# RWKV5 attention and SwiGLU on one core: an opening in another order, a hint for the closing branch, and six closing stores

## The chip, the cores and the metric

The kernel runs on one NeuronCore of a Trainium2 chip. The metric is the device time of one execution in microseconds (us). The five engines named below are PE (matrix multiply), PEld (its weight loads), DVE (vector), ACT (scalar), POOL (GpSimd) and SP, which here only issues DMA transfers. Each engine takes its instructions strictly in the order of its own queue and waits on semaphores for the others.

## The reference

Two blocks stand one behind the other. The first is an RWKV5 attention over 4 batches, 8 heads, 768 steps and head size 48:

```python
for t in range(S):
    kt, vt, rt = k[:, :, t], v[:, :, t], r[:, :, t]
    cur = einsum('bhd,bhe->bhde', u[None] * kt, vt)
    y[:, :, t] = einsum('bhd,bhde->bhe', rt, state + cur)
    state = w[None, :, :, None] * state + einsum('bhd,bhe->bhde', kt, vt)
```

The result is laid out as x, 3072 tokens by 384 columns, and goes through a SwiGLU feed-forward with 1536 hidden columns:

```python
g = x @ w_gate
out = (g / (1 + exp(-g)) * (x @ w_val)) @ w_out
```

The three weight matrices arrive as 64-bit floats; r, k, v, w and u are 32-bit.

## The kernel before

**Items.** The sequence is cut into six chunks of 128 steps. With four batches that makes 24 items; item i is chunk i // 4 of batch i % 4. In each item the recurrence becomes matrix products: keys and receptances are scaled by powers of the decay w and turned (transposed) by PE, their product gives a 128 by 128 score matrix for each head (`scores`, L454), a mask keeps its strict triangle, the diagonal gets the products of r, u and k (`diagonal`, L364 on ACT and L371 on POOL), and `outputs` (L507) multiplies the scores with v, and the turned receptances with the state. `update` (L522 on PE, L532 to L535 on DVE and POOL) carries the state to the next chunk.

**The scalings.** DVE works out two tables of powers in turned layout. For items 0 to 3 PE turns the raw k and r and DVE multiplies by the tables on the way out of PSUM (L387). The same tables are turned back once (`natural_tables`, L349) and kept by ACT (`keep_natural_tables`, L353); with them POOL scales keys and receptances in natural layout (`scale_k` L341, `scale_r` L344), and the later items are turned after scaling and copied by ACT (L389). The products of r, k and u for the diagonal are made on POOL (`own_begin` L254, `own_end` L257) and summed on DVE (`own_sum` L265).

**The weights.** They come in 18 chunks of 768 KB (`load_weights`, L179), first and second alternately from w_gate and w_val, then w_out. Each is rounded from 64 to 32 bits by ACT (`round_high` L199, `round_low` L205), DVE (`round_dve` L214 and L215) and POOL (`add_low` L223, or `round_pool` L242 for a whole chunk).

**The feed-forward.** Gate and value units (L545) start as soon as a first pair of weight chunks is rounded and two items have their outputs; `feed` runs them between the attention's steps. Sums over weights and activations are used to save products; the closing part ("tail") consists of `three_units` (L801 on PE) and `project_thirds` (L1027 on PE, evictions L1020 and L1022), whose last pieces store the rows to the output (L995).

**What sets the order.** The scheduling is manual: the function `fast` writes out the program, and the order of calls is the order in each engine's queue. What the tile pools leave open is only waiting. SP's queue issues nearly all loads, one behind the other, so a load that waits for a buffer holds up all loads behind it. The opening, from `load(0)` to the loop over s, is written out call by call. `warm(n)` puts n identity products on PE; each is recorded as two matmuls.

**The end.** At the twelfth step the kernel counts the values of w outside the range that its tables can take, and leaves the count in `outside`. After `fast`, each of the five engines loads this count into a register (L1375) and compares and branches (L1376): where the count is above zero, a general version of the whole kernel, whose code stands between, is run; here it is zero, and the branch jumps over that code. Behind it SP waits for the others and the closing barrier ends the program.

Of the kernel before, what the change touches and what calls it, by code (L numbers as in the profile page):

```python
# [15 lines left out]
P = 128  # L16
# [6 lines left out]
def fast(  # L23
# [24 lines left out]
    nc = tc.nc  # L48
# [7 lines left out]
    DM, DFF = moe_w_gate.shape  # L56
# [86 lines left out]
    def load_v(i):  # L143
        c, b = divmod(i, B)
        for e in range(2):
            for p, a, o in places(i, HP):
                rows = slice(P * c + p.start + o, P * c + p.stop + o)
                sp.dma_start(
                    out=v_ld[i % 4][p, a, 64 * e : 64 * e + D],
                    in_=v[b, :, rows, :].rearrange("(a e) t d -> e t a d", e=2)[e][:, a],  # L150
                )
# [22 lines left out]
    def load_weights():  # L174
        n = next_chunk("load")
        if n is not None:
            src = chunks[n][0].bitcast(INT32)
            bits[n] = three.tile([P, WN, 2], INT32, name="w_bits", tag="w_bits")
            sp.dma_start(  # L179
                out=bits[n][:].rearrange("p (c f) two -> p c (f two)", c=src.shape[1]), in_=src  # L180
            )
# [81 lines left out]
    def own_sum(i):  # L263
        dus[i] = three.tile([P, H], FP32, name="du", tag="du")
        dve.tensor_reduce(dus[i][:], rks.pop(i), axis=AX.X, op=ALU.add)  # L265
# [18 lines left out]
    load(0)  # L284
    load(1)
    load_weights()
    load_v(0)
    load_weights()
    load_v(1)

    act.activation(sg0[:], ident[:, 0:1], AF.Silu)
    def warm(n, bank=None):

        ps = next_psum(HP, P)[:, 0, :] if bank is None else bank[:, 0:P]
        for _ in range(n):
            pe.matmul(ps, ident[:], ident[:], start=True, stop=True)  # L296

    warm(12)
    u_ps = next_psum(CC, P).rearrange("p c t -> p (c t)")
    pe.matmul(u_ps, ones_row, u_row, start=True, stop=True)  # L300
    act.copy(ub.rearrange("p h d -> p (h d)"), u_ps)
    next_psum(CC, P)
    warm(4)

    pool.memset(mask[:], 1.0)
    pool.affine_select(
# [39 lines left out]
    def natural_tables():  # L346
        for bank, t in zip(banks, (pw[:, :, 1 : P + 1], pv)):
            for a in range(HP):
                pe.transpose(bank[:, P * a : P * a + P], t[:, a, :], ident[:])  # L349
# [29 lines left out]
    def turn(i):  # L379
        kr = khat[i % 4], rhat_of(i)  # L380
        tps = [next_psum(HP, P) for _ in kr]
        turned[i] = three.tile([P, HP, P], FP32, name="rT", tag="rT")
        for tp, t, dst, table in zip(tps, kr, (kT[i % 2], turned[i]), (pw[:, :, 1 : P + 1], pv)):
            for a in range(HP):
                pe.transpose(tp[:, a, :], pair(t, a), ident[:])  # L385
            if i < 4:
                dve.tensor_mul(dst[:], tp[:], table)  # L387
            else:
                act.copy(dst[:], tp[:])  # L389
# [569 lines left out]
    def project_thirds(g):  # L959

        ends = g + 2 == N // 2
        A, B_, C, D_, E, F = room["h"]
        (x00, x01), (x10, x11), (x20, x21) = (
            [third(hTs, k, j) for j in range(2)] for k in range(3)
        )
        h = {
            "r3": A, "r4": B_, "r1": C, "r0": D_, "r8": E, "r10": F, "r14": A, "r13": B_,
            "r12": C, "r2": D_, "r6": E, "r5": x00, "r7": x21, "r9": x20, "r11": x11,
        }
        rows = hv[:, NR + 6 : NR + 12].rearrange("p (q r) t -> p q (r t)", q=2)  # L970
        c = [rows[:, :, DM * (k % 2) + P * (k // 2) :][:, :, 0:P] for k in range(6)]
        made = {
            0: [(dve.tensor_sub, E, x01, x11)],
            1: [(dve.tensor_add, F, x01, x21)],
            2: [(dve.tensor_add, A, x10, x20)],
            3: [(dve.tensor_sub, B_, x00, F)],
            4: [(dve.tensor_add, C, B_, x20)],
            5: [(dve.tensor_sub, D_[q], D_[q], x20[:, q]) for q in range(2)],
            6: [(dve.tensor_add, E[:, q], D_[q], x21[:, q]) for q in range(2)],
        }  # L980
        used = {
            "r3": [("copy", 2)], "r4": [("copy", 1)], "r1": [("copy", 0)], "r0": [("sub", 2)],
            "r8": [("copy", 3), ("sub", 1)], "r10": [("copy", 5)], "r14": [("copy", 4)],
            "r12": [("add", 0)], "r13": [("add", 4)], "r2": [("add", 5)], "r6": [("add", 3)],
            "r9": [("sub", 4)], "r5": [("sub", 0), ("sub", 1)], "r11": [("add", 2), ("add", 3)],
            "r7": [("add", 5)],
        }
        lasts = ("r4", "r0", "r8", "r9", "r5", "r11", "r7")
        open_ = {}

        def store(q, j):
            cc, b = divmod(2 * (g + q) + j, B)
            n0 = S * b + P * cc
            issue = sp if ends and q == 0 else act
            issue.dma_start(out=out[n0 : n0 + P, :], in_=rows[:, q, DM * j : DM * j + DM])  # L995

        def make(n):
            for op, o, a, b in made.get(n, ()):
                op(o, a, b)
            if not ends:  # L1000
                prepare_threes(g + 2, n)

        def item(n):
            what, chain = THIRDS[n]
            if n:
                make(n)
            first = chain not in open_
            split = ends and chain == "l5"
            if first:
                open_[chain] = [take()] + ([ring_a.popleft()] if split else [])  # L1010
            banks_ = open_[chain]

            def evict(q):
                for how, k in used[what]:
                    x = banks_[0][:, 0 : 2 * P].rearrange("p (q t) -> p q t", q=2)
                    if split:
                        x = banks_[q][:, q * P : q * P + P]
                    o = c[k][:, q] if split else c[k]
                    if how == "copy":
                        act.copy(o, x)  # L1020
                    else:
                        (dve.tensor_add if how == "add" else dve.tensor_sub)(o, o, x)  # L1022

            for q in range(2):
                ps = banks_[q if split else 0][:, q * P : q * P + P]
                for f in range(4):
                    pe.matmul(  # L1027
                        ps, (h[what][q] if h[what] is D_ else h[what][:, q])[:, f, :], wide["o"][what][:, f, :],
                        start=first and f == 0 and (split or q == 0), stop=f == 3, skip_group_check=True,
                    )  # L1030
                if split:
                    evict(q)
                    if what == "r7":
                        store(q, 1)
            if not split:
                evict(None)
            if n == 0:
                for do in wide.pop("last"):
                    do()
                make(0)  # L1040
            if what in lasts:
                free.append(banks_[0])
            if what == "r11":
                store(0, 0)
                store(1, 0)
            if what == "r7" and not split:
                store(0, 1)
                store(1, 1)
        return [lambda n=n: item(n) for n in range(15)]
# [149 lines left out]


    turn(0)
    own_sum(0)
    own_begin(1)
    diagonal(0)
# [1 line left out]
    flush()  # L1206
    load(2)
    turn(1)
    natural_tables()
    round_high(0, 0, 0)  # L1210
    round_low(0)
    load(3)
# [14 lines left out]
    add_low(1, 0)  # L1227
    own_product(2)
    outputs(1)
    keep_natural_tables()  # L1230
    scale_k(0)
    scale_k(1)
    queue(0)
# [4 lines left out]
        del bits[n], lows[n]  # L1238
    done.update(act=2, pool=2)
    load_weights()  # L1240
    turn(2)
    feed(1)
    own_sum(2)
    diagonal(2)
    flush()
    own_product(3)
    turn(3)
    dve.tensor_copy(w128[:].unsqueeze(2), pw[:, :, 0:1])
    warm(3, free[0])
    scores(2)  # L1250
    update(0)
    update(1)
    feed(1)
    own_sum(3)
    diagonal(3)
    flush()
    scores(3)
    scale_k(2)
    outputs(2)
    load(4)  # L1260
    round_act()
    scale_k(3)
    outputs(3)
    round_act()
    round_pool()
    update(2)
    update(3)
    scale(4)
    load_v(4)
    feed(1)  # L1270
    round_pool()
    own_product(4)
    load(5)
    feed(1)
    own_sum(4)
    round_act()
# [80 lines left out]
    tail = threes[0] + projections[0][:-2]  # L1357
    tail += threes[1][0:1] + projections[0][-2:-1] + threes[1][1:2] + projections[0][-1:]
    tail += threes[1][2:] + projections[1]
    for piece in tail:  # L1360
        piece()


@with_exitstack
def kernel(
    ctx: ExitStack,
    tc: tile.TileContext,
    *args: bass.AP,
):
    nc = tc.nc  # L1370
    ctx.enter_context(tc.manual_schedule())
    flag = ctx.enter_context(tc.tile_pool(name="flag", bufs=1))
    outside = flag.tile([1, 1], INT32, name="outside")
    fast(tc, *args, outside[:])
    n = nc.values_load(outside[:], min_val=0, max_val=512)  # L1375
    with tc.If(n > 0):  # L1376
        general(tc, *args)


# [395 lines left out]
```

## Time and profile before

| | us |
|---|---|
| median of 3 runs (lowest, highest) | 595.56 (594.47, 597.43) |
| the profiled execution | 594.87 |
| its span on the core | 593.1 |
| PE busy | 580.1 |
| PEld busy | 521.0 |
| DVE busy | 421.7 |
| POOL busy | 355.1 |
| ACT busy | 225.8 |

The mean clock granted to PE was 0.997 of full speed. The span runs from the first to the last record of the core; the execution's own time is 1.8 us longer.

Lines of the profile are read as follows. A line of the timeline gives the start, the length, the engine, the line of the kernel, the operation, output and inputs by name, shapes and a count of merged instructions; the bracket at its end gives the idle time of that engine just before, and the instruction that ended it. An engine's name followed by q stands for its sequencer: the issue of a DMA, a register load, a branch or a semaphore wait. In the page's slices each digit is the busy share of one fortieth of the span, in tenths. The chain is followed back from the last instruction to what released each one.

### The profile page before, as it was taken

Reading aid. Unit: us, or ns where it says so; the run is one execution under the profiler, and the core shown is the slowest. Engines: PE = TensorE matmul, PEld = TensorE weight load, DVE = VectorE, ACT = ScalarE, POOL = GpSimd, SP = SyncE. Lnnn points to the kernel's source line nnn. Section 1 sums busy time; section 2 is a strip of 40 time slices with the busy share of each in tenths; the row PEclk is TensorE's granted clock in tenths of the full one; section 3 lists DMA queues with packets and bytes.
Section 4 is the critical chain, followed back from the end, with each engine's and each line's share of the span. In section 5 each row is a group of like instructions: output and inputs, shape, how many; then the busy total and the mean of one; then the engine's idle time right before and its main releaser. Section 6 shows DMA issues by size and latency. Waiting matters only on the chain.

```text
span 593.1 us, 13229 instructions
## 1 busy us (share of the span) xinstructions
PE 580.1 (98%) x5234; PEld 521.0 (88%) x5234; DVE 421.7 (71%) x703; ACT 225.8 (38%) x517; POOL 355.1 (60%) x378
## 2 busy tenths in 40 slices
PE   8989999999999999999999999999999999999995
PEld 7778888899888899988899988889988899988895
DVE  7867887489488877577887477779257877377672
ACT  3468886321343422244332344423134320233310
POOL 6789889989999503977601996513678960010600
PEclk9999999999999999999999999999999999999998
DMA  8979887732342323233234233200100000100001
GB/s 198 254 177 252 236 287 87 86 65 48 75 74 35 54 48 68 49 62 57 39 60 82 60 54 54 48 12 3 54 1 1 1 1 1 55 0 1 1 2 59
DMA packets 148009, 41.53 MB, mean 70 GB/s; under 512 B 138465, under 2 KB 141794, under 8 KB 147938
## 3 DMA queue, kind: packets, MB, share of 16 engines
q1 hardware_dynamic: 144770, 36.27, 30.4%
q10 hardware_dynamic: 3168, 4.33, 2.0%
q8 instruction: 43, 0.70, 0.5%
q14 instruction: 28, 0.23, 0.1%
HBM read 28.31 MB, written 4.72 MB: 56 GB/s over the span
## 4 chain that ended last, share of the span: by engine, by line
PE 88%; POOL 4%; DVE 2%; SPq 2%; DMA 1%; issue 1%; ACT 1%; POOLq 0%; DVEq 0%
PE bank L801 28%; PE bank L620 18%; PE ring L801 13%; PE bank L1027 9%; PE bank L545 8%; PE ring L507 5%; PE ring L454 3%; SPq L411 2%; POOL wgv L242 1%; POOL s L731 1%; PE ring L522 1%; PE ring L296 1%; PE ring L385 1%; DMA r_ld<-in_r_dram 1%; POOL hats L344 0%
## 5 line engine op out<-in xcount | busy, mean ns | idle before, releaser
L825 DVE TENSOR_TENSOR hv<-hv,bank 128x512 f32<-128x512 f32 x132 | 87.1, 681 | 25.7 <-PE bank L801 14.8
L545 PE MATMUL bank<-xT,wgv 128*128 128x256 f32 x288 | 66.3, 384 | 0.0
L801 PE MATMUL bank<-xf,wgv 128*128 128x256 f32 x256 | 65.9, 382 | 0.0
L364 ACT ACTIVATE At<-ident,du 128x128 f32<-128x128 f32 x176 | 59.8, 396 | 14.8 <-DVE du L265 6.4
L825 ACT COPY hv<-bank 128x512 f32<-128x512 f32 x72 | 40.1, 585 | 58.6 <-PE bank L801 52.3
L545 PEld LDWEIGHTS bank<-xT,wgv 128*128 128x128 f32 x288 | 53.4, 190 | 8.2 <-issue 0.2
L731 POOL TENSOR_TENSOR s<-wgv 128x256 f32<-128x256 f32 x39 | 29.9, 789 | 48.6 <-PE bank L620 48.5
L801 PEld LDWEIGHTS bank<-xf,wgv 128*128 128x128 f32 x256 | 47.8, 190 | 7.0 <-DVE kT L1069 0.6
L1078 POOL TENSOR_TENSOR hv<-At,hats 128x512 f32<-128x512 f32 x8 | 10.2, 1275 | 66.0 <-ACT At L1077 66.0
L535 POOL TENSOR_TENSOR Z<-Z,w 48x192 f32<-48x192 f32 x32 | 16.9, 527 | 36.5 <-DVE Z L534 35.3
L507 PE MATMUL ring<-At,v_ld 128*32 128x128 f32 x768 | 35.6, 273 | 3.1 <-DVE At L464 3.1
L832 ACT ACTIVATE hv<-hv 128x512 f32<-128x512 f32 (+1 forms) x33 | 21.3, 668 | 45.8 <-DVE hv L825 45.6
L801 PE MATMUL bank<-xT,wgv 128*128 128x256 f32 x144 | 35.9, 382 | 0.2 <-DVE hv L825 0.2
L801 PE MATMUL bank<-xT,s 128*128 128x256 f32 x152 | 35.5, 380 | 0.2 <-POOL s L731 0.2
L507 PEld LDWEIGHTS ring<-At,v_ld 128*32 128x32 f32 x768 | 30.5, 110 | 4.8 <-DVE At L464 4.7
L620 PE MATMUL bank<-wt,hs 128*128 128x192 f32 x192 | 33.7, 328 | 0.6 <-DVE hs L594 0.6
L620 PE MATMUL bank<-wo,hs 128*128 128x192 f32 x192 | 33.9, 327 | 0.0
L620 PE MATMUL bank<-wo,hv 128*128 128x192 f32 x192 | 33.4, 327 | 0.0
L801 PEld LDWEIGHTS bank<-xT,s 128*128 128x128 f32 x152 | 28.6, 190 | 5.0 <-issue 0.6
L620 PEld LDWEIGHTS bank<-wt,hs 128*128 128x128 f32 x192 | 31.3, 190 | 1.4 <-ACT At L364 0.8
L620 PEld LDWEIGHTS bank<-wo,hv 128*128 128x128 f32 x192 | 31.6, 190 | 0.4
L620 PEld LDWEIGHTS bank<-wo,hs 128*128 128x128 f32 x192 | 31.6, 190 | 0.3
(226 smaller groups left out, 1397.5 us busy)
## 6 DMA issues: line engine op xcount, KB each, us to landing
hats<-hats SPq DMA_DIRECT2D x192, 32.0 KB, 2.0
w_bits<-in_moe_w_gate_dram SPq DMA_DIRECT2D x6, 768.0 KB, 6.2
w_bits<-in_moe_w_val_dram SPq DMA_DIRECT2D x6, 768.0 KB, 6.0
w_bits<-in_moe_w_out_dram SPq DMA_DIRECT2D x6, 768.0 KB, 6.7
out_dram<-hv ACTq DMA_DIRECT2D x22, 192.0 KB, 1.9
v_ld<-in_v_dram SPq DMA_DIRECT2D x24, 96.0 KB, 5.4
k_ld<-in_k_dram SPq DMA_DIRECT2D x8, 192.0 KB, 3.8
r_ld<-in_r_dram SPq DMA_DIRECT2D x8, 192.0 KB, 4.3
```

Of the source, the lines that this page charges most:

```text
L364: lambda h=h: act.activation(At[i % 2][:, h, :], ident[:], AF.Identity, scale=du[:, h : h + 1])
L411: sp.dma_start(out=bass.AP(tensor=dst.tensor, offset=dst.offset, ap=[list(dst.ap[0]), [-P, 2 * HP], [1, 32]],), in_=bass.AP(tensor=src.ten ...
L454: pe.matmul(ps[e][keys, a, cols], kT[i % 2][rows, at(i, a), keys], turned[i][rows, at(i, a), cols], start=True, stop=True, skip_group_chec ...
L507: pe.matmul(ps[32 * q : 32 * q + 32, cc, :], *x, start=start, stop=stop, skip_group_check=True,)
L535: pool.tensor_mul(ze, ze, w)
L545: pe.matmul(gv[:, o, :].rearrange("p (i t) -> p i t", i=2), wt[:, c, P * f : P * (f + 1)], xT[:, 2 * g % NX : 2 * g % NX + 2, c, :], start ...
L620: pe.matmul(ps, lhs[:, f, :], rhs[:, f, :], start=(f == 0 and n in (0, 1, 4)), stop=(f == FH - 1), skip_group_check=True,)
L731: op(made[o], made[a], made[b])
L801: pe.matmul(ps[:, o], u[:, o], v, start=first and o == 0, stop=True, skip_group_check=True,)
L825: do(out, *(pair_of(wide[a][:]) if isinstance(a, str) else a for a in args))
L832: todo.append((at, lambda: act.activation(gate, gate, AF.Silu)))
L1027: pe.matmul(ps, (h[what][q] if h[what] is D_ else h[what][:, q])[:, f, :], wide["o"][what][:, f, :], start=first and f == 0 and (split or ...
```

## The change

Nothing that is computed for the output is changed. Two parts of the program are put in another order, some warming products go, and the end gets a hint and more, smaller stores.

**In the opening.** On SP the second chunk of weights (the first of w_val) is issued ahead of the loads of v for item 0, and `load(4)` and `load(5)` stand together, directly behind the third call of the weights' loads and ahead of the further ones. On PE the warming goes from twelve and four calls to five and two, and a third place with three calls goes altogether; the eight transposes of `natural_tables` stand ahead of the second item's turn. On ACT the two copies of `keep_natural_tables` stand ahead of the first rounding. On DVE the copy of `w128` stands behind the first turn rather than the fourth, the multiplies of `turn(2)` stand ahead of the roundings of the second halves of the first two chunks, and `own_sum(3)` ahead of a feed-forward unit's multiply. On POOL the `scale_k` and `scale_r` of item 4 and its own product stand ahead of what they followed: `scale_k(4)` ahead of the third item's diagonal L371, the other two ahead of two whole-chunk additions (L242).

**At the end.** Each engine's load of the count into a register, with SP's register operations and range assertion, stands ahead of the tail's first piece rather than behind the last store. A branch prefetch hint tied to the closing branch is put into the stream of each of the five engines; in the built program it stands as the first instruction of the engine's main block. The last two row blocks are stored in two parts: columns 0 to 255 together with the stores of the first two blocks' rows, the last 128 columns where the whole was stored. There are six stores, three on SP and three on ACT, rather than four.

```diff
     load(0)
     load(1)
     load_weights()
+    load_weights()
     load_v(0)
-    load_weights()
     load_v(1)
...
-    warm(12)
+    warm(5)
...
     next_psum(CC, P)
-    warm(4)
+    warm(2)
...
-        def store(q, j):
+        def store(q, j, a=0, z=DM):
...
-            issue.dma_start(out=out[n0 : n0 + P, :], in_=rows[:, q, DM * j : DM * j + DM])
+            issue.dma_start(out=out[n0 : n0 + P, a:z], in_=rows[:, q, DM * j + a : DM * j + z])
...
                     if what == "r7":
-                        store(q, 1)
+                        store(q, 1, 2 * P)
...
             if what == "r11":
                 store(0, 0)
                 store(1, 0)
-            if what == "r7" and not split:
+                if ends:
+                    store(0, 1, 0, 2 * P)
+                    store(1, 1, 0, 2 * P)
+            if what == "r7" and not ends:
                 store(0, 1)
                 store(1, 1)
...
     turn(0)
+    natural_tables()
+    dve.tensor_copy(w128[:].unsqueeze(2), pw[:, :, 0:1])
     own_sum(0)
...
     turn(1)
-    natural_tables()
+    keep_natural_tables()
     round_high(0, 0, 0)
...
     outputs(1)
-    keep_natural_tables()
+    turn(2)
     scale_k(0)
...
     load_weights()
-    turn(2)
+    load(4)
+    load(5)
     feed(1)
...
     turn(3)
-    dve.tensor_copy(w128[:].unsqueeze(2), pw[:, :, 0:1])
-    warm(3, free[0])
     scores(2)
     update(0)
     update(1)
+    scale_k(4)
+    own_sum(3)
     feed(1)
-    own_sum(3)
     diagonal(3)
...
     outputs(2)
-    load(4)
     round_act()
     scale_k(3)
     outputs(3)
+    scale_r(4)
     round_act()
+    own_product(4)
     round_pool()
     update(2)
     update(3)
-    scale(4)
     load_v(4)
     feed(1)
     round_pool()
-    own_product(4)
-    load(5)
     feed(1)
...
+    n = nc.values_load(outside, min_val=0, max_val=512)
+    tc.mark_branch_hint_location("general", engines=list(mybir.ALL_ENGINES))
     for piece in tail:
         piece()
+    return n
...
-    fast(tc, *args, outside[:])
-    n = nc.values_load(outside[:], min_val=0, max_val=512)
-    with tc.If(n > 0):
+    n = fast(tc, *args, outside[:])
+    with tc.If(n > 0, label="general"):
         general(tc, *args)
```

## The prediction

> **What bounds the kernel now.** I read the page's slices and chain first, then the table of busy times by stage, then the PE's timeline at the head and every record of the last 10 us.
>
> ```profile
> span 593.1 us, 13229 instructions
> PE   8989999999999999999999999999999999999995
> PE 88%; POOL 4%; DVE 2%; SPq 2%; DMA 1%; issue 1%; ACT 1%; POOLq 0%; DVEq 0%
> ```
>
> PE carries the chain. What PE does not carry sits in the first two slices and the last. By stage (columns: length, then busy us of PE, PEld, DVE, ACT, POOL, then clock, DMA share, GB/s):
>
> ```profile
> 0.00:20.00 20.00, 16.85 (x169) 14.46 (x170) 13.82 (x36) 9.61 (x21) 12.52 (x24) 1.00 0.83 195
> 20.00:40.00 20.00, 18.32 (x290) 15.68 (x289) 16.62 (x34) 8.60 (x21) 16.18 (x16) 1.00 0.89 215
> 40.00:60.00 20.00, 18.82 (x192) 15.79 (x192) 14.19 (x29) 16.85 (x41) 19.69 (x18) 1.00 0.96 251
> 60.00:100.00 40.00, 40.00 (x462) 34.65 (x461) 32.82 (x67) 31.68 (x75) 33.98 (x31) 1.00 0.75 212
> 580.00:594.00 14.00, 7.09 (x64) 6.89 (x62) 2.77 (x8) 0.00 (x0) 0.00 (x0) 0.83 0.18 62
> ```
>
> From 60 us on PE is full (199.97 of 200 between 100 and 300), so whatever the head gains before 60 us arrives undiminished at the end. PE's holes there, from its timeline (start, length, work, in brackets the idle time and who ended it):
>
> ```profile
> 12.86 0.41 PE L507 MATMUL ring<-At,v_ld 128*32 128x128 f32 x4
> 18.55 2.83 PE L545 MATMUL bank<-xT,wgv 128*128 128x256 f32 x12
> 33.77 5.45 PE L545 MATMUL bank<-xT,wgv 128*128 128x256 f32 x24
> 42.84 0.66 PE L385 MATMUL ring<-ident,hats 128*128 128x128 f32 x4 [0.16 <-POOL hats L341]
> 43.81 0.66 PE L385 MATMUL ring<-ident,hats 128*128 128x128 f32 x4 [0.31 <-POOL hats L344]
> 56.40 0.43 PE L507 MATMUL ring<-rT,Z 112*32 112x128 f32 x8 [0.72 <-ACT kT L389]
> ```
>
> Counted from start to start, less the usual spacing, the three bracketed holes are 0.32, 0.47 and 0.88 us. And the end:
>
> ```profile
> L1375 SPq TENSOR_LOAD <-outside x1: 772/772/772, 587.0 to 587.0; - x1
> L1376 SPq COMPARE_BRANCH  x1: 45/45/45, 588.2 to 588.2; - x1
> L1376 SPq EVENT_SEMAPHORE  x8: 17/17/17, 591.2 to 591.8; - x8
> L1376 PEldq COMPARE_BRANCH  x1: 3782/3782/3782, 585.5 to 585.5; - x1
> 587.12 0.29 DVE L1022 TENSOR_TENSOR hv<-hv,ring 128x128 f32<-128x128 f32 x1 [0.60 <-PE ring L1027]
> 587.44 0.34 ACTq L995 DMA_DIRECT2D out_dram<-hv  x1
> ```
>
> SP's branch takes 45 ns, but its next instruction starts 3.0 us later (588.2 to 591.2); DVE and ACT show the same hole. The last store, issued at 587.44, landed at 590.61, before SP resumed. So today the branch, not the store, sets the end, with SP's waits and the closing barrier behind it (591.2 to 593.1, 1.9 us).
>
> [...] 3.0 us on SP, 3.78 on PE, and two 16 KB instruction packets (1.24 and 1.34 us) at 586.47 and 589.97. [...] here starts are 0.213 us apart up to 5.40 us (3.96 us after the first matmul) and 0.112 after. [...]
>
> **Part 1, the opening.** PE's warm-up loses nine calls (18 records). The u matmul came at 6.22; five cold calls end near 3.7, so it comes near 3.8 and ub near 5.1 instead of 7.17. POOL's second own product of item 0 then ends near 7.0 (was 7.79), and the first key turn waits for DVE's tables (ready 7.56) rather than PE: its DVE multiply moves from 8.69 to about 7.6. Against this, w_val's 768 KB now precede v(0) in SP's queue. v(0) landed at 12.20 and 12.61, w_val near 14.55: 1.94 us for those bytes. So v(0) lands near 14.2 to 14.6, and the first L507 matmul goes from 12.86 to about 14.4, +1.5. Its copy to xT delays ACT's L199 of chunk 1 (15.43 to 16.3) and POOL's add_low (17.55 to 18.0). The first gate unit moves from 18.55 to about 18.95: a loss of 0.4, with bounds 0 and 1.5, the latter if nothing behind outputs absorbs it. If PE stays cold, 24 transposes at 0.107 extra are at most 2.6, mostly under DVE; taken 0. The two ACT table copies (0.44 each) move ahead of round_high, where ACT waits on nothing needed earlier: 0. The moved natural transposes (eight, 1.04 us) lie where PE waits: 0. The moved w128 copy may cost 0.2 to 0.9 on DVE; it is hidden by the v(0) wait.
>
> **Part 2, 19 to 34 us.** warm(3) goes (0.75), and turn(2)'s two multiplies precede DVE's roundings, so rT2 is ready near 19.3 instead of 22.65. The second gate unit (25.26) starts about 0.9 earlier. But POOL is busy without a hole from 18 to 27.5 with additions, own products and L371, all of which remain, and it begins them 0.45 later. It then sat idle 2.09 us until own_sum(3) released At(3) at 29.60; own_sum(3) is now a place earlier on DVE, but scale_k(4) (0.98) stands ahead of At(3) on POOL. The 0.75 and 0.9 gained on PE are thus mostly waited away at At(2) and At(3): of 2.09, about 0.98 is filled and 0.45 eaten by the later start, leaving some tenths. The unit at 33.77 I put near 33.65: net of Part 1 up to here 0.1, bounds -0.5 and +0.5.
>
> **Part 3, 34 to 60 us.** scale_k(4), scale_r(4) and own_product(4) fill POOL's holes of 2.09 us (27.5 to 29.6) and 1.66 (32.6 to 34.3), ahead of two 1.8 us L242 additions. k5 and r5, issued at 40.78 and 41.20 and landed at 44.71 and 45.55, are now issued behind load(4): SP's three waits move earlier, and what they pass is a 768 KB chunk needed at 39.6, which lands near 33.7. POOL's hats for item 5 end near 41.0 instead of 43.75, so the two holes before turn(5), 0.32 + 0.47 = 0.79, close. The 0.88 at 56.40 stands behind the chain POOL L242, ACT L205 (0.92, which waited 1.29), ACT kT L389; with POOL 2.7 us ahead it closes to between 0.55 and all: 0.8. Head sum: 0.1 + 0.79 + 0.8 = 1.7; bounds 0.3 and 2.5.
>
> **Part 4, the load of the flag.** Five TENSOR_LOADs move ahead of the tail (about 429 us). On DVE, ACT and POOL, which have slack there, 0. On PE 0.489 us stands in its instruction stream behind some 80 small L507 matmuls; PE's sequencer is barely ahead of its array there (a wait at 430.97, its matmul at 431.01), so 0 to 0.5; I take +0.3. At the end SP's load, FUSED_REGOPS and SEQ_ASSERT (1.1 us, 587.0 to 588.16) are gone.
>
> **Part 5, branch hint and six stores.** The hint is emitted at the start of each engine's stream, some 590 us ahead of its branch. If it holds, [...] the 3.0 us hole goes. What is late next is the last store. It is now 64 KB rather than 192, issued at the same 587.44. 192 KB stores elsewhere land in 1.87 to 1.9 us; these four took 3.2 to 3.9 because three shared the queues and one DMA engine carried a 16 KB fetch. So it lands at 589.05 to 589.5. Waits already passed shorten the 1.9 to 1.3 to 1.9: end near 590.9 of 593.1, gain 2.2 (1.7 to 2.7). If the hint does nothing, SP still branches at 587.0 instead of 588.16: gain 1.1, and the stores are hidden anyway. Two more issues (0.35 to 0.6 each) lie on SP and ACT before the last eviction: 0.
>
> **The sum.** Against the profiled execution's 594.87 (span 593.1 and 1.8 around it): -1.7 - 2.2 + 0.3 = -3.6, so 591.3. The median shown, 595.56, is 0.7 above it: 592.0.
>
> **Rivals.** (a) *The hint does nothing*: armed 590 us early, [...] Against: it is tied to the named branch. -1.7 - 1.1 + 0.3 = -2.5, 593.1. (b) *The head gives nothing*: late v(0) and POOL's unbroken 18 to 27.5 us swallow it, and the POOL lead is spent by other waits. For: the first unit is later. Against: the holes at 43 and 56 have one named releaser each. 0 - 2.2 + 0.3, about 593.7. (c) *Slower*: [...] Each exposed fetch costs about 3.0 us, as the branch does; with -2.5 otherwise, two exposed on PE decide for slower (+3.5, 599), one makes it even. For: nothing in this profile shows a hint. Against: PE's queue of ready work is deep, and no hole in its stream now comes from fetching. Late v(0) alone (+1.5) cannot do it.
>
> **How the numbers follow.** Both gains 0.55 at 592.0, own range 590.5 to 593.2; hint idle 0.25 at 593.1; head empty 0.12 at 593.7; slower 0.08 at 599. About 0.5%, 2.98 us, is what a measurement of this kernel can tell from none: below 592.58 is faster, above 598.54 slower. By the spread of their terms some three quarters of the first case (0.41), and two fifths of the idle hint (0.10) and of the empty head (0.05) fall below: faster 0.56, slower 0.08, the rest 0.36. The range takes 589.9 (both gains at their better bounds) to 595.4 (head lost to late v(0), hint idle).
>
> **What would show it.** Right: SP's first wait behind the branch within 0.3 us of it, no instruction packet after 586 us, the last store landed before 589.6; no hole over 0.2 before turn(5) and at 56; the first L545 unit near 18.95, the one at 33.77 near 33.65. Wrong: a first unit later than 19.5, new PE holes over 1 us without a releaser (fetching), or the 3 us hole still there.

## The result and the profile after

The changed kernel takes 592.13 us (median of six runs, 591.40 to 592.92), against 595.94 us for the kernel before in the same comparison: a ratio of 0.9939 with a 95% interval of 0.992 to 0.9959. A second comparison, made beside the experiments, gave 592.09 against 595.08, 0.9958 (0.994 to 0.9976). The ratios, here and below, are the record's own estimate over all executions of a comparison; they are not the quotient of the two medians, from which they differ by up to 0.0015, or 0.9 us. The gain is thus 2.5 us (second ratio) to 3.8 us (first medians). The profiled execution of the first comparison took 591.40 us, the lowest of its six, with a span of 589.7.

The page of the changed kernel: span, PE's slices, the chain's shares by engine.

```profile
span 589.7 us, 13188 instructions
PE   8999999999999999999999999999999999999996
PE 93%; DVE 1%; ACT 0%; issue 0%; DVEq 0%; ACTq 0%
```

POOL's 4% and SP's 2% have left the chain. The stages, in the same columns as before (length; busy us of PE, PEld, DVE, ACT, POOL; clock, DMA share, GB/s):

```profile
0.00:20.00 20.00, 16.93 (x153) 14.07 (x154) 15.71 (x39) 9.64 (x21) 12.89 (x24) 1.00 0.88 211
20.00:40.00 20.00, 17.96 (x286) 15.22 (x285) 15.39 (x33) 9.44 (x22) 19.44 (x19) 1.00 0.99 244
40.00:60.00 20.00, 20.00 (x200) 17.38 (x199) 16.21 (x33) 17.76 (x46) 18.32 (x18) 1.00 0.97 226
60.00:100.00 40.00, 40.00 (x472) 34.48 (x471) 31.28 (x63) 31.72 (x76) 34.43 (x30) 1.00 0.83 209
580.00:594.00 14.00, 4.17 (x38) 3.98 (x36) 2.08 (x6) 0.00 (x0) 0.00 (x0) 0.92 0.17 59
```

PE is full from 40 us on, not from 60, and POOL's busy time between 20 and 40 us rose from 16.18 to 19.44. The same work is done with fewer holes, and earlier. PE's timeline of the opening:

```profile
13.58 1.62 PE L507 MATMUL ring<-At,v_ld 128*32 128x128 f32 x32 [0.84 <-DMA v_ld<-in_v_dram]
18.12 2.75 PE L545 MATMUL bank<-xT,wgv 128*128 128x256 f32 x12
32.96 5.45 PE L545 MATMUL bank<-xT,wgv 128*128 128x256 f32 x24
53.90 0.43 PE L507 MATMUL ring<-rT,Z 112*32 112x128 f32 x8
```

The first outputs now wait for v, which is new, and the longest hole, PE's wait for At near 30 us, is 1.94 us from start to start instead of 1.51. The three bracketed holes of before, at 42.84, 43.81 and 56.40, are gone: the work that started at 56.40 starts at 53.90. At the end, the branch (L1381 here), the closing stores and the last eviction:

```profile
L1381 SPq EVENT_SEMAPHORE  x8: 17/17/17, 587.8 to 588.3; - x8
L1381 PEldq COMPARE_BRANCH  x1: 397/397/397, 582.0 to 582.0; - x1
L1381 SPq COMPARE_BRANCH  x1: 70/70/70, 585.4 to 585.4; - x1
L995 ACTq DMA_DIRECT2D out_dram<-hv x7: 338/445/1620, 504.5 to 584.9; - x7
L995 SPq DMA_DIRECT2D out_dram<-hv x3: 372/406/1545, 582.9 to 585.0; - x3
584.21 0.29 DVE L1022 TENSOR_TENSOR hv<-hv,ring 128x128 f32<-128x128 f32 x1 [0.61 <-PE ring L1027]
```

PE's branch takes 0.40 us instead of 3.78. SP branches at 585.4 and is now held until 587.8 by a store: its first wait passes at 587.77, and the last store lands at 587.93. The columns of the two store rows are minimum, median and maximum length of one issue in ns. On each queue one issue took over 1.5 us, where before the two of SP took 0.36 and 0.37. So the last stores were issued at 584.93 and 584.99, 0.4 to 0.5 after the last eviction was done, and took 2.8 and 2.9 us to land.

The profiled executions differ by 3.47 us (594.87 to 591.40), their spans by 3.46. The difference has three parts. At 56 us PE is 2.50 ahead. At 380 us it is 3.30 ahead (380.08 against 376.78), because two waits of 0.36 us, from start to start less the usual spacing, of the kernel before, at 361.07 for DVE and at 372.88 for POOL, did not appear; 0.4 of this is lost at 515.46, where PE starts behind ACT's copy to y (L1072), and the last eviction is 2.91 ahead. From the last eviction's end to the end of the span it takes 5.2 us instead of 5.7: the end itself brought only some 0.5.

### The profile page after: what moved, and what is told of

Its sections match the earlier page's. It is cut to its first block, busy times and chain, and to the rows that moved or that the text cites. A ratio compares the mean times of both kernels' runs of the same rounds, so it can differ in the third digit from the quotient of the medians.

```text
span 589.7 us, 13188 instructions
## 1 busy us (share of the span) xinstructions
PE 578.3 (98%) x5210; PEld 519.7 (88%) x5210; DVE 421.0 (71%) x703; ACT 225.6 (38%) x517; POOL 355.5 (60%) x378
## 4 chain that ended last, share of the span: by engine, by line
PE 93%; DVE 1%; ACT 0%; issue 0%; DVEq 0%; ACTq 0%
PE bank L801 31%; PE bank L620 18%; PE ring L801 13%; PE bank L545 10%; PE bank L1027 9%; PE ring L507 6%; PE ring L454 3%; PE ring L522 1%; PE ring L385 1%; DVE hv L825 0%; PE ring L1027 0%; DVE hs L594 0%; ACT At L364 0%; DVE hs L593 0%; DVE At L464 0%
## 5 line engine op out<-in xcount | busy, mean ns | idle before, releaser
L507 PE MATMUL ring<-At,v_ld 128*32 128x128 f32 x768 | 35.6, 273 | 3.4 <-DVE At L464 2.5
L507 PEld LDWEIGHTS ring<-At,v_ld 128*32 128x32 f32 x768 | 30.5, 110 | 5.0 <-DVE At L464 4.5
```

What stands on the lines that cost most here:

```text
L507: pe.matmul(ps[32 * q : 32 * q + 32, cc, :], *x, start=start, stop=stop, skip_group_check=True,)
```

## The experiments

No experiment leaves out any part of the computation. In each, "last eviction to end" is the span less the end of the last L1022 eviction.

**The two halves apart.** The end alone, put on the kernel before:

```diff
+    n = nc.values_load(outside, min_val=0, max_val=512)
+    tc.mark_branch_hint_location("general", engines=list(mybir.ALL_ENGINES))
     for piece in tail:
         piece()
...
+                if ends:
+                    store(0, 1, 0, 2 * P)
+                    store(1, 1, 0, 2 * P)
```

> The kernel before with the end of the changed kernel alone (hint, loads of the flag ahead of the tail, six stores). Theory A, from the two traces (the end gained 0.6 us, the rest came from PE's stream): 0.4 to 1.0 us under the kernel before; SP's first wait behind the branch no longer 3.0 us late; the last store lands 3.2 to 3.5 us after the last eviction. Theory B, the split of the prediction (end 2.2, opening 1.7): 1.9 to 2.5 us under it, the last store landing within 2.1 us of the last eviction.

Measured: 594.34 against 594.81, ratio 0.9984 (0.9969 to 0.9999): 0.5 us less by the medians, 0.95 by the ratio. Last eviction to end is 4.9 us; the last store lands 3.2 us after the eviction. Theory A.

The opening alone is the changed kernel with the end of before (the diff above reversed).

> The changed kernel with the end of the kernel before (no hint, loads of the flag behind the tail, four stores). Theory A: 2.5 to 3.0 us under the kernel before, the PE stream 2.5 ahead at the first L507 after 50 us, and the end as before (3.0 us hole behind SP's branch). Theory B: 1.2 to 1.8 us under it.

Measured: 592.69 against 594.81, 0.9964 (0.9955 to 0.9973), 2.1 us less: between the two theories' ranges. PE is 2.34 ahead at the first L507 after 50 us, and last eviction to end is 6.0 us. The halves add: 0.9984 times 0.9964 is 0.9948, between the two comparisons of the whole. Some 70% (ratios) to 80% (medians) of the gain are the opening's.

**The hint.** Only the hint goes; the loads of the flag stay ahead of the tail, and there are six stores.

```diff
-    tc.mark_branch_hint_location("general", engines=list(mybir.ALL_ENGINES))
...
-    with tc.If(n > 0, label="general"):
+    with tc.If(n > 0):
```

> The changed kernel without the branch hints. Theory A (hint removes the fetch, but the last store then sets the end): the hole of 3.0 us comes back behind SP's branch at about 585.4, SP resumes near 588.4 instead of 587.8, span 590.2 to 590.6 against 589.7. Theory B (the hint was worth its 3.0 us less the store): span 590.8 to 591.3. Theory C (the hint does nothing, another part closed the hole): span 589.7 and no hole.

Measured: 593.17 against 594.81, 0.9975 (0.9966 to 0.9985). The branch's rows of this kernel (L1380):

```profile
L1380 SPq EVENT_SEMAPHORE  x8: 17/17/17, 591.2 to 591.8; - x8
L1380 PEldq COMPARE_BRANCH  x1: 3671/3671/3671, 584.3 to 584.3; - x1
L1380 SPq COMPARE_BRANCH  x1: 45/45/45, 587.5 to 587.5; - x1
```

The holes are back: 3.67 us on PE, and on SP 3.8 us from the branch (587.46) to the next instruction (591.23), 0.7 longer than in the kernel before. The instruction packet of 16 KB behind the branch is back too (at 589.11, where the kernel before has it at 589.97), while the changed kernel has none behind SP's branch. Theory C, that the hint does nothing, is out. Last eviction to end is 6.3 us against 5.0 in the changed kernel's second profile, so the hint is worth 1.3 us there, and about 1.0 by the medians (593.17 against 592.16 for the four stores below, on the same chip; the two differ in the stores too). The span of 593.1 missed every theory's number, but not because of the end: this execution, the second longest of its twenty, lost 2 us in the opening, as told below. Set behind the changed kernel's last eviction (584.50), the 6.3 us would end at 590.8, the low end of theory B. The end without the hint is also no better than the old end: 593.17 against 592.69 with the new opening and the old end, and 6.3 us from the last eviction against 6.0. So neither the six stores nor the earlier loads of the flag show a gain of their own; what the end gained is, by these traces, the hint's.

**Four stores or six.** The changed kernel with four closing stores of 192 KB:

```diff
-                        store(q, 1, 2 * P)
+                        store(q, 1)
...
-                if ends:
-                    store(0, 1, 0, 2 * P)
-                    store(1, 1, 0, 2 * P)
-            if what == "r7" and not ends:
+            if what == "r7" and not split:
```

> The changed kernel with four closing stores of 192 KB. Theory A1 (the six stores crowd: four issues within 0.5 us stall each other for 1.5 us, and gain nothing): the stores' issues take under 0.5 us each, the last lands 3.0 to 3.4 us after the last eviction, span 589.3 to 589.8. Theory A2 (the smaller last store helps although it lands late): the last store lands 3.7 us or more after the last eviction, span 590.1 to 590.6.

Measured: 592.16 against 594.81, 0.9957 (0.9943 to 0.9971). Last eviction to end is 4.5 us, and the last store, though three times as large, lands 3.0 us after the eviction. That is theory A1 on this point, while the span of 590.8 is outside its range through a slower opening (the last eviction ended at 586.30). Its issues:

```profile
L995 ACTq DMA_DIRECT2D out_dram<-hv x6: 338/347/444, 506.3 to 586.3; - x6
L995 SPq DMA_DIRECT2D out_dram<-hv x2: 373/624/876, 584.7 to 585.5; - x2
```

The longest issue on SP is 0.88 us instead of 1.55, and ACT's last 0.34. So fewer stores were held for less time here. "Under 0.5 us each" was too low. By the ratios, 0.9957 against 0.9958 and 0.9939, four stores are not told from six.

**The changed kernel once more**, as the yardstick for the runs beside it:

> The changed kernel once more, as the yardstick of the runs beside it. 3.3 to 4.0 us under the kernel before if its first comparison holds; 2.5 to 2.9 if it equals the sum of the end alone and the opening alone.

Measured: 592.09 against 595.08, 3.0 us less by the medians and 2.5 by the ratio, nearer to the sum of the halves. PE is 1.91 ahead at 56 us rather than 2.50, and last eviction to end is 5.0 us. Its opening:

```profile
14.26 1.37 PE L507 MATMUL ring<-At,v_ld 128*32 128x128 f32 x32 [1.04 <-DMA v_ld<-in_v_dram]
18.93 0.66 PE L385 MATMUL ring<-ident,hats 128*128 128x128 f32 x4 [0.61 <-DMA hats<-in_r_dram]
19.42 2.75 PE L545 MATMUL bank<-xT,wgv 128*128 128x256 f32 x12
33.55 2.64 PE L545 MATMUL bank<-xT,wgv 128*128 128x256 f32 x11
```

The same program has its first unit at 18.12 in one execution and 19.42 in another. The first half of v of item 0 landed at 13.45 in the first and 14.12 in the second, and the receptances of item 2 behind it held PE only in the second. The transfers of the first 20 us are not the same twice, so one trace of this opening does not give its price.

**v ahead of w_val**, as it was:

```diff
     load_weights()
-    load_weights()
     load_v(0)
+    load_weights()
     load_v(1)
```

> The changed kernel with v of item 0 ahead of w_val in SP's queue, as before. Theory A (w_val's 2.1 to 2.4 us ahead of v are waited for at the first outputs, and only partly given back): the first L507 matmul near 12.6 to 12.9, its wait named At and no longer the load, PE at the first L507 after 50 us 0.3 to 0.8 earlier, time 0.3 to 0.8 us under the changed kernel. Theory B (w_val earlier is what brings the first gate units forward, so undoing it loses): first L545 unit later than 18.4, time 0.3 to 1.0 above the changed kernel. Theory C: POOL and DVE set the unit at 33 us either way, within 0.3.

Measured: 591.28 on the chip where the changed kernel takes 592.09, 0.9951 (0.9932 to 0.9971) against before.

```profile
12.40 1.62 PE L507 MATMUL ring<-At,v_ld 128*32 128x128 f32 x32
15.29 0.41 PE L507 MATMUL ring<-At,v_ld 128*32 128x128 f32 x4 [1.26 <-DVE At L464]
17.84 1.46 PE L545 MATMUL bank<-xT,wgv 128*128 128x256 f32 x6
```

The first outputs start at 12.40 without a wait for v, and PE at the first L507 after 50 us is at 53.53 (53.90 and 54.49 in the changed kernel's two profiles). The sizes are theory A's: 0.8 us by the medians, though 0.4 by the ratios, and the two intervals overlap. The same swap with four stores (last experiment) is worth 0.0004 of the ratio, some 0.2 us, and its profile doesn't show the gain: the scores start late, at 11.63, the first outputs at 13.72, and the first L507 after 50 us at 54.83. So the gain is likely, not settled. Theory B is not borne out: without w_val's early place the first unit starts at 17.84 here and at 19.18 there, within or below the changed kernel's 18.12 to 19.42.

**Items 4 and 5 as before** (their scalings, own product and loads):

```diff
     load_weights()
-    load(4)
-    load(5)
     feed(1)
...
-    scale_k(4)
     own_sum(3)
...
     outputs(2)
+    load(4)
     round_act()
     scale_k(3)
     outputs(3)
-    scale_r(4)
     round_act()
-    own_product(4)
     round_pool()
     update(2)
     update(3)
+    scale(4)
     load_v(4)
     feed(1)
     round_pool()
+    own_product(4)
+    load(5)
```

(In the kernel `own_sum(3)` keeps its new place ahead of `feed(1)`.)

> The changed kernel with the scalings, the own product and the loads of items 4 and 5 where they were before (part 3 of the prediction undone). Theory A (that part is worth 0.79 before turn(5) and about 0.8 at 56 us): the two waits of PE for POOL's L341 and L344 near 42 us come back with 0.6 to 0.9 together and the wait for ACT's L389 with 0.6 to 1.0; time 1.3 to 1.9 us above the changed kernel. Theory B (the earlier second half of the opening already clears them): no such waits, time within 0.5.

Measured: 593.93, by the medians 1.84 us above the changed kernel on the same chip; 0.9982 (0.9969 to 0.9995) against before, by the ratios 1.4 us. The lowest of its twelve times, 593.46, lies above the highest of the changed kernel's five, 592.45.

```profile
42.48 0.66 PE L385 MATMUL ring<-ident,hats 128*128 128x128 f32 x4 [0.18 <-POOL hats L341]
43.45 0.66 PE L385 MATMUL ring<-ident,hats 128*128 128x128 f32 x4 [0.30 <-POOL hats L344]
56.08 0.43 PE L507 MATMUL ring<-rT,Z 112*32 112x128 f32 x8 [0.76 <-ACT kT L389]
```

All three holes come back at their old places with their old releasers: from start to start, less the usual spacing, 0.34, 0.46 and 0.92 us, 1.72 together. Theory A. This one part is worth about half of the whole gain, or more.

**The middle of the opening as before**: turn(2), own_sum(3) and three warming calls.

```diff
     outputs(1)
-    turn(2)
     scale_k(0)
...
     load_weights()
+    turn(2)
     load(4)
...
     turn(3)
+    warm(3, free[0])
     scores(2)
...
-    own_sum(3)
     feed(1)
+    own_sum(3)
```

> The changed kernel with turn(2), own_sum(3) and the three warming calls where they were before (part 2 of the prediction undone). Theory A (own_sum(3) ahead of the unit's multiply brings At(3) forward by its own 0.4 and the warming by 0.75; about 0.8 at the unit at 33 us): outputs(3) and that unit 0.6 to 0.9 later, time 0.6 to 1.0 us above the changed kernel. Theory B (the prediction's 0.1; POOL sets it anyway): within 0.3.

Measured: 593.07 against 594.56, 0.9972 (0.996 to 0.9984).

```profile
31.86 0.41 PE L507 MATMUL ring<-At,v_ld 128*32 128x128 f32 x4 [1.19 <-DVE At L464]
34.16 2.21 PE L545 MATMUL bank<-xT,wgv 128*128 128x256 f32 x9
```

The unit that stands at 33.55 in the changed kernel's second profile stands at 34.16 here, 0.6 later, with v of item 0 landing 0.3 earlier. The ratios differ by 0.0014, or 0.8 us. That is theory A's size, across two chips and with intervals that overlap.

**The warming as before**, twelve and four calls instead of five and two:

```diff
-    warm(5)
+    warm(12)
...
-    warm(2)
+    warm(4)
```

> The changed kernel with twelve and four warming calls instead of five and two. Theory A (the wait for v and w_val covers the start of the opening): first scores 1.0 to 1.3 later, the first L507 matmul within 0.3, time within 0.3 us of the changed kernel. Theory B (the earlier turns are worth their 1.1): 0.7 to 1.2 above.

Measured: 593.17 against 594.56, 0.9974 (0.9965 to 0.9982), with single times from 591.96 to 595.17. The trace speaks for theory A: the first outputs are at 14.17 (14.26 in the changed kernel's second profile), and the span is 590.4 (590.2). But the scores, at 11.33 (11.04), are only 0.3 later, not 1.0 to 1.3. The ratio speaks for theory B, some 0.95 us above. The profiled execution, 592.26, is among its five lowest, so it does not show what the median holds. Five of the 22 executions have a mean clock of 0.995 or less; without them the median is 592.96, so a loss of clock explains only 0.2 of it. This stays open.

The new places of `natural_tables`, `keep_natural_tables` and the copy of `w128` were not undone alone; what each is worth is not shown.

**Earlier closing stores.** The rows' columns become final in three steps, so they can leave in three steps before the last. The changed kernel with eight stores:

```diff
+            if ends and what == "r9":
+                store(0, 0, 2 * P)
+                store(1, 0, 2 * P)
+            if ends and what == "r5":
+                pair_store(0, 0)
+                pair_store(1, 0)
+            if ends and what == "r11":
+                pair_store(0, P)
+                pair_store(1, P)
-            if what == "r11":
+            if what == "r11" and not ends:
                 store(0, 0)
                 store(1, 0)
-                if ends:
-                    store(0, 1, 0, 2 * P)
-                    store(1, 1, 0, 2 * P)
```

`pair_store(q, a)` writes columns a to a + 127 of two neighbouring row blocks with one transfer.

> The changed kernel with the closing rows stored in eight stores as their columns become final: columns 256 to 383 of the first block pair behind r9, columns 0 to 127 of both behind r5, columns 128 to 255 of both behind r11, the last 128 columns behind r7. 393 KB instead of 786 are left for the last 1.8 us. Theory A (the stores queued together delay the last one): the last lands 1.9 to 2.4 us after the last eviction instead of 3.2 to 3.5, span 1.0 to 1.5 shorter from the last eviction to the end than the 5.2 of the changed kernel. Theory B (a last store takes 3 us whatever else is queued): 3.0 or more after it, and no gain; with more stores, a loss of 0.3.

Measured: 591.75 against 595.08, 0.9951 (0.9933 to 0.997). Last eviction to end is 4.3 us, 0.7 less than the changed kernel's 5.0 on that chip. SP's last store lands 2.4 us after the eviction, although its issue still took 1.52 us. For ACT's last store, issued at 587.08, the trace has no landing; SP passes its third wait at 589.63, 2.6 us after the eviction, and waits no longer for a store behind it. Direction and landing are theory A's, a little late; the 1.0 to 1.5 were not reached: from 589.63 the rest of SP's sixteen waits and the barrier take another 1.7. The profiled execution (593.08, span 591.4) was slow in its opening, and shows how. Columns as in the table of stages, first this kernel, then the changed kernel's first profile:

```profile
30.00:35.00 5.00, 3.36 (x98) 2.89 (x99) 4.18 (x8) 4.49 (x11) 4.92 (x6) 0.79 0.89 216
35.00:40.00 5.00, 5.00 (x22) 4.29 (x21) 3.18 (x8) 0.75 (x2) 5.00 (x4) 0.87 1.10 339
```

```profile
30.00:35.00 5.00, 4.13 (x105) 3.57 (x106) 4.78 (x9) 4.30 (x9) 4.92 (x6) 1.00 0.69 222
35.00:40.00 5.00, 5.00 (x29) 4.45 (x28) 3.53 (x10) 1.88 (x4) 5.00 (x4) 1.00 1.07 317
```

PE's mean clock fell to 0.79 and 0.87 of full speed in these two stretches. It was at half speed for 3.41 us; the clock stands third from the end:

```profile
32.93:36.34 3.41, 3.41 (x73) 2.93 (x64) 3.13 (x7) 2.15 (x4) 3.33 (x4) 0.50 0.95 296
```

In PE's timeline of the eight stores the same pieces are longer:

```profile
32.87 1.58 PE L522 MATMUL ring<-v_ld,hats 128*32 128x48 f32 x58
34.38 6.40 PE L545 MATMUL bank<-xT,wgv 128*128 128x256 f32 x24
```

The updates take 1.58 us instead of 0.93 and the 24 matmuls 6.40 instead of 5.45: 1.6 us lost. The kernel without the hint, whose edit is 550 us away, shows the same (0.79 and 0.86; half speed from 32.95 to 36.36), so the stores are not the cause. Both had PE's two longest holes in this place among the new openings, 1.94 and 2.12 us from start to start, less the usual spacing.

**Both repairs together**, v ahead of w_val and the eight stores:

> The changed kernel with both repairs: v of item 0 ahead of w_val, and the closing rows stored in eight stores as their columns become final. The two gains, 0.8 and about 0.7 (4.3 us from the last eviction to the end instead of 5.0), add: 590.3 to 590.8, 4.3 to 4.8 us under the kernel before. If the early stores cost PE or DVE something, no more than the 0.8.

Measured: 591.58 against 594.56, 0.9946 (0.9932 to 0.996). Its profiled execution is the shortest of all, 590.50 with a span of 588.8, and last eviction to end is again 4.3 us:

```profile
583.70 1.41 SPq L995 DMA_DIRECT2D out_dram<-hv  x1
584.24 0.29 DVE L1030 TENSOR_TENSOR hv<-hv,ring 128x128 f32<-128x128 f32 x1 [0.60 <-PE ring L1035]
584.56 0.55 ACTq L995 DMA_DIRECT2D out_dram<-hv  x1
```

ACT's last store is issued 0.03 us after the eviction. The median is 3.0 us under the kernel before, not the 4.3 to 4.8 expected. It is the lowest ratio of the experiments, but the first comparison of the changed kernel, 0.9939, lies below it, so "better than the changed kernel" is likely by the trace, not shown by the times. Nor do the two gains show as a sum: 0.9946 is 0.3 us under the eight stores alone (0.9951).

**v ahead of w_val with four stores**:

> The changed kernel with v of item 0 ahead of w_val and four closing stores of 192 KB instead of six. If the six stores crowd (4.5 us from the last eviction to the end with four, 5.0 with six): 0.3 to 0.6 under the kernel with v first and six stores, thus 590.7 to 591.1. If the 4.5 was chance: 591.3 or more, and 5.0.

Measured: 592.06 against 594.56, 0.9953 (0.994 to 0.9966): the 590.7 to 591.1 were missed. Last eviction to end is 4.7 us, so the four stores' 4.5 was not all chance, but one SP issue took 1.26 us here too. Six, four and eight stores give 4.9 to 5.2 (seven traces with the hint), 4.5 and 4.7, and twice 4.3. Dividing the last two blocks, as the change does, thus did not shorten the end in any trace; only the stores that leave earlier did.

## Why the prediction was right, and where it was not

The time was predicted at 592.0 and measured at 592.13. The total is right; its split is not. The opening brought more and the end much less. That two wrong terms cancelled so well is luck, and the second comparison, 3.0 us by its medians instead of 3.6, agrees less closely. The lower end of the stated range, 589.9, does not come out of the bounds either: 595.56 less 2.5 and 2.7 is 590.4.

**Parts 1 and 2.** The first key multiply came at 7.64, as worked out (about 7.6). POOL's second product was put to end near 7.0 instead of 7.79. But 7.79 was its start in the kernel before; it now began at 7.17 and took 1.33 us, so that term was too early by the product's own length. The case that PE stays cold, taken at 0, came true: its matmuls of 128 by 128 start 0.213 us apart until 9.10 and 10.16 in the two profiles, instead of until 5.40 (in the first, those of L349 and L385 behind it start 0.11 apart). The first scores start at 10.56 and 11.04 nevertheless, against 10.77 before. v was put at 14.2 to 14.6 and landed at 13.45 and 14.12; the first unit was put at 18.95 and came at 18.12 and 19.42, the one at 33.65 at 32.96 and 33.55. The prediction's values lie inside the spread or up to 0.1 past its late end. The copy of `w128`, put at 0.2 to 0.9, took 0.33 us at 9.16, with POOL's L254 beside it until 9.46; before, it took 0.94 at 24.56, beside POOL's L371. What sets its length was not shown. Undoing the two steps gives, within the noise, 0.2 to 0.8 lost by w_val ahead of v (0.4 assumed), and about 0.8 won by turn(2), own_sum(3) and the missing third warming (0.5 implied by the net 0.1). Neither is clear of its term.

**Part 3** was right in mechanism and size: 0.79 and 0.8 predicted, 0.80 and 0.92 of holes and 1.4 to 1.84 us of time when undone.

**Part 4.** The term of +0.3 for PE's register load was mis-sized. PE's load (0.61 us, at 425.14) cost nothing: PE was 3.30 ahead at 380 us and 3.29 at 470. The lower bound held. The two waits that vanished near 361 and 372 us were not foreseen, and come and go: the opening alone has both (at 358.93 and 370.94), the second profile of the changed kernel neither.

**Part 5** holds the step that failed: "it lands at 589.05 to 589.5", and with it the gain of 2.2. That the hint holds was right; "what is late next is the last store" was right too. Its lateness was mis-sized. I gave it the 1.87 to 1.9 us of stores that travel alone, from an issue right at the eviction, and laid the longer landings of before on shared queues and an instruction packet, an inference from one trace. The runs showed an issue 0.1 to 0.5 late, held by the issues ahead of it, and a landing 2.8 to 3.1 us after the issue: 3.2 to 3.4 from the eviction, no better than the 3.2 of before. "Two more issues ... 0" was wrong for the same reason. The end gained 0.5 (trace) to 0.95 (ratio of the end alone) rather than 2.2. Two of the signs for "right" showed it: SP's first wait passed 2.3 us behind the branch, not within 0.3, and two instruction packets of 8 KB still came at 586.83 and 586.87. The third, a last store landed before 589.6, was met at 587.93 although the step failed, since the whole program was 2.9 us earlier; tied to the last eviction it would have been missed.

**Rivals.** (a), an idle hint, given 0.25 by the author's estimate, falls with the holes of 3.0 to 3.8 us that return without it on SP, PE, DVE and ACT. Its price was wrong as well: without the hint the end took 6.3 us from the last eviction, 0.6 more than before, where a gain of 1.1 was put. (b), an empty opening, falls with the opening alone at 0.9964. (c), fetch holes on PE, was an estimate from the 3.0 us of SP's branch and was not seen: no new hole over 1 us in PE's stream lacked a releaser. The sum held because a stream of PE underrated by 0.8 to 1.5 us (parts 1 to 4: 1.4 predicted, 2.18 and 2.91 at the last eviction of the two profiles) met an end overrated by 1.3 to 1.7. Of the 0.8 to 1.5, the opening has 0.2 to 0.8 (1.91 and 2.50 at 56 us against 1.7), part 4's term 0.3, and the waits that come and go the rest.

## What to carry to other kernels

When a wait is taken away, price the next one with everything that is queued beside it: a store's landing alone (1.9 us) says little about the last of six issued within 2 us. Splitting the last transfer helped here only where what stands ahead of it left earlier (4.3 us from the last eviction to the end with eight stores, 4.9 to 5.2 with six, 4.5 and 4.7 with four). And where an opening is set by loads, compare several executions or undo one part at a time: one trace had the same unit 1.3 us earlier than another of the same program.

## What the runs showed of the hardware

The hint stands 581 (PE) to 585 us (SP) ahead of its branch and still works: 0.40 us instead of 3.64 to 3.78 on PE, and about half a microsecond from branch to next instruction on DVE and ACT, where it was 3.2 to 3.3 before. Each hint takes 0.05 us.

Most issues of an output store of 64 to 192 KB take 0.34 to 0.47 us. But of the six closing stores, the two issued within 0.5 us of the first two took 1.16 to 1.62 in every trace. With four stores one took 0.88 and 1.26 behind the new end, and none over 0.37 in the two profiles with the old end. Of four 192 KB stores on ACT's queue alone, near 510 us, the last took 0.69 to 1.15 in three traces and 0.44 in the others. The held closing issues ended 1.6 to 2.1 us after the first of their group. What they wait for, the traces don't name.

PE was at half clock for 3.41 us near 33 us in two profiles of the new opening, in neither of the two of the old one. It need not be the new opening's own: like these two executions, 16 of the 102 of the kernel before that were timed with the experiments have a mean clock of 0.995 or less. Where in these the clock was lost, the record doesn't show. In the 3.41 us before the loss, PE was busy for 1.32 and 1.50 us. The first profile of the changed kernel has 1.53 in the 3.41 us from 28.00 and keeps its clock, and holes of 1.91 and 1.93 us in two profiles did not lose it either. Between those that lost it and those that kept it lie as little as 0.03 us of busy time and 0.01 us of hole, so what takes the clock is not shown.
